# Rests of the first and the last unit multiplied as a second pair, and a new order of the last stores

## The chip, the cores and the metric

The kernel runs on one core of a Trainium2 chip. The core has five engines that run side by side, each through its own instructions in order: TensorE (PE in the profile; its weight loads are PEld), VectorE (DVE), ScalarE (ACT), GpSimd (POOL) and SyncE (SP), which here issues nearly all DMA transfers. They wait for one another by semaphores. The metric is the device time of one execution in microseconds; lower is better.

## The reference

The program is an attention block with normalized queries and keys, followed by a feed-forward layer with a squared ReLU, all in float32.

```python
batch, n_heads, seq, head_dim = (8, 12, 448, 64)
n_tokens, d_model, d_ff = (3584, 768, 2048)

def rmsnorm(x, g):
    rms = np.sqrt(np.mean(x * x, axis=-1, keepdims=True) + 1e-06)
    return x / rms * g
q_n, k_n = (rmsnorm(q, g_q), rmsnorm(k, g_k))
scores = scale * np.matmul(q_n, k_n.transpose(0, 1, 3, 2))
attn = softmax(scores)                    # written out with max, exp and sum
x = np.matmul(attn, v)                    # then (B, H, S, D) -> (B*S, H*D)
h = np.maximum(x @ w_in, 0.0)
out = h * h @ w_out
```

## The kernel before

**Units, blocks, stages.** Two batches (2 x 448 = 896 rows) make a unit; there are four, u = 0 to 3. The feed-forward layer of unit u runs while the attention of unit u+1 is computed; unit 3's runs alone at the end. The hidden width of 2048 is cut into four blocks. A block of a unit has *first products* (x @ w_in, then ReLU and square into the tiles `hid`) and *second products* (`hid` @ w_out, added into the accumulators `accs`).

**Seven products for eight.** Matrix products are done by Winograd's form of Strassen's method: four quarters are multiplied in seven products (P1 to P7, table `PRODUCTS`) of sums of quarters. In the second products of a unit, the 448 rows of one batch and the 448 of the other are the two row halves. A row tile has 128 rows, so each batch gives NT = 3 whole tiles, and the three pairs of tiles (tt = 0, 1, 2) are multiplied by `product(tt, name, ...)`: two matmuls of 128x384 (t = 0, 1) into a bank of PSUM, then one eviction (two for P7) by VectorE or ScalarE into the accumulators. The banks are three, in `roles`, turned from tile to tile. A bank is free for its next product when its eviction is done. The sums of hidden quarters (S1, S2, S4 and the changed S3) are made by POOL in `hidden_sum`, those of t = 0 during the first products, the rest after them (`make_sums`).

**Rests.** What is left of each unit is a tile of 64 + 64 rows, its *rest*. Units 1 and 2 (`KEPT`) store theirs to DRAM (`keep_rests`), and unit 3 loads both (`bring_rests`), forms their sums (`add_rests`) and multiplies them as a fourth pair, tt = NT, at the end of each block: seven products. The rests of units 0 and 3 are multiplied alone by `multiply_rest` (L1159 to L1171): eight matmuls a block. In unit 0 they come straight after the first products, under the last activations and the four POOL sums; in unit 3 they stand among the products of tile 0 (`FIRST_OF_BLOCK`).

**What sets the order.** All engines' instructions are issued in the order in which the Python code makes them. `ffn(u)` is a generator that yields a cost after each product: COST_IN = 18 for a first product of unit 0, COST_OUT = 10 for a second product. The main loop computes attention in *visits*, 24 in a unit's stage, and runs the generator between them until its summed cost reaches `place(u, x)`: in unit 0 at equal shares of COST. A visit ends in exponentials on ScalarE; the query and key transposes for the next pair (L367, on VectorE, each waiting for a transfer) are queued half a visit before.

**Weights.** In unit 0's stage the weights also have to be converted. They come as 64-bit words: `all_pieces` lists 64 pieces, per block eight `in` pieces (for the first products) and eight `out` pieces. A piece is loaded by SP into one of three buffers `words`, split by ScalarE in three steps (L1405, L1406, L1408), and joined by VectorE in two (L1419, L1438). After four pieces, sums of weight quarters are made by VectorE and POOL in turn (L1514). Each call of `convert()` joins the previous piece and splits the next; `early` and `late` list the costs at which it is called. A load is queued two steps of the generator after the conversion two pieces earlier. The derived weights for later units go to DRAM (`in_deep`, L1464, L1466, L1492) and are loaded again by `load_piece` (L892), eight or nine of these loads at the end of unit 0's last first products.

**First products of unit 0.** Seven products, twice a block, with six records each (L986). The results of P1, P5, P6 and P4 are copied by ScalarE (L995) into `part`, since the next product adds to the same bank: the copy of P1 has to be done before P6, that of P5 before P3, that of P6 before P7.

**Stores.** `store` (L1346) writes whole accumulators to `out` in the last block; in unit 3 the accumulators of tt = NT are written last, as four transfers of 64 rows.

## Time and profile before

| What | us |
|---|---|
| median of 3 runs (1391.83 to 1393.26) | 1392.92 |
| the profiled execution's own time | 1394.38 |
| its span | 1392.6 |
| stage of unit 0 (125.0 to 486.2) | 361.2 |
| stages of units 1 and 2 (486.2 to 800.0, to 1102.5) | 313.8, 302.5 |
| stage of unit 3 (to 1385.1) | 282.6 |
| from the last matmul to the end of the span | 7.5 |

A line of the profile names the source line, the engine, the operation, out<-in by the program's names, shapes and count. A timeline line begins with start and duration in us; brackets at its end hold the engine's idle time before it and what ended it. A line of waits has the waiting engine and line, what it waited for, then us in all, times and the longest. A line by stretches has start:end, its length, then busy us and instructions of PE, PEld, DVE, ACT and POOL, the granted TensorE clock, the share of time that the DMA engines were busy, and GB/s. [...] The granted clock was 1.00 in the stages of units 0, 2 and 3 and 0.99 in that of unit 1.

### The profile page before, as it was taken

How to read it: one execution, taken by the hardware profiler on the slowest of the kernel's cores; microseconds unless marked ns; L12 is line 12 of the kernel's file. 1: busy time of each engine (PE TensorE's matmuls, PEld its weight loads, DVE VectorE, ACT ScalarE, POOL GpSimd, SP SyncE). 2: the span in 40 equal slices, each digit the busy share in tenths (PEclk: the TensorE clock that was granted, in tenths of full speed). 3: DMA queues.
4: the chain of work that ended last, by engine and by line, in shares of the span. 5: the costliest groups of instructions: out<-in, count | busy, mean ns of one | idle time of the engine just before them, and what ended most of it. 6: DMA issues, size and time to landing. Idle time of an engine off the chain costs nothing.

```text
span 1392.6 us, 19474 instructions
## 1 busy us (share of the span) xinstructions
PE 1363.3 (98%) x6320; PEld 845.7 (61%) x6320; DVE 807.2 (58%) x1635; ACT 608.3 (44%) x1118; POOL 789.6 (57%) x794
## 2 busy tenths in 40 slices
PE   7999999999999999999999999999999999999997
PEld 3333444444444466676758586676768677868684
DVE  4786545867758755555556755455546642445444
ACT  6885477757666244353434244442434032202020
POOL 5668664746656868576667877566745630303030
PEclk9999999999999999999999999999999999999999
DMA  5566746968769875664739475755527442424223
GB/s 147 149 168 169 203 117 159 264 179 219 233 155 284 231 215 162 187 173 141 204 86 279 140 225 149 211 153 176 146 86 239 142 165 103 135 90 149 78 90 100
DMA packets 385588, 233.36 MB, mean 168 GB/s; under 512 B 272452, under 2 KB 354244, under 8 KB 381380
## 3 DMA queue, kind: packets, MB, share of 16 engines
q1 hardware_dynamic: 385184, 231.95, 57.7%
q8 instruction: 52, 0.85, 0.3%
q14 instruction: 60, 0.49, 0.1%
q10 hardware_dynamic: 292, 0.07, 0.0%
HBM read 174.59 MB, written 57.34 MB: 167 GB/s over the span
## 4 chain that ended last, share of the span: by engine, by line
PE 81%; POOL 4%; DVE 4%; DMA 3%; issue 3%; SPq 2%; ACT 2%; POOLq 0%; ACTq 0%; DVEq 0%
PE bank L1251 30%; PE bank L1042 20%; PE bank L986 8%; PE bank L446 5%; PE bank L536 5%; PE bank L550 4%; PE bank L435 4%; PE bank L1165 2%; POOL sum L473 2%; PE bank L585 1%; DMA qk<-in_k_dram 1%; PE bank L611 1%; SPq L326 1%; SPq L318 1%; PE bank L571 1%
## 5 line engine op out<-in xcount | busy, mean ns | idle before, releaser
L1042 PE MATMUL bank<-xT,in_sb 128*128 128x224 f32 x1344 | 289.3, 354 | 2.9 <-ACT part L1031 2.3
L1251 PE MATMUL bank<-out_sb,hid 128*128 128x384 f32 x768 | 272.5, 488 | 2.2 <-POOL out_sb L1514 1.4
L1345 DVE TENSOR_TENSOR acc<-acc,bank 128x384 f32<-128x384 f32 x312 | 166.6, 548 | 164.6 <-PE bank L1251 138.1
L1042 PEld LDWEIGHTS bank<-xT,in_sb 128*128 128x128 f32 x1344 | 252.6, 190 | 15.0 <-ACT wT L454 5.6
L454 ACT ACTIVATE wT<-bank,rr 128x448 f32<-128x448 f32 x288 | 163.5, 631 | 155.1 <-PE bank L435 92.7
L1251 PE MATMUL bank<-out_sb,sums 128*128 128x384 f32 x576 | 207.2, 490 | 1.3 <-DVE acc L1345 0.9
L1251 PEld LDWEIGHTS bank<-out_sb,hid 128*128 128x128 f32 x768 | 144.7, 190 | 104.5 <-issue 5.6
L204 POOL TENSOR_TENSOR rr<-ms,minus_half 128x8 f32<-128x8 f32 (+1 forms) x96 | 146.0, 1521 | 73.7 <-DVE ms L197 63.8
L1251 PEld LDWEIGHTS bank<-out_sb,sums 128*128 128x128 f32 x576 | 107.7, 190 | 86.3 <-issue 4.3
L1027 DVE TENSOR_TENSOR hid<-hid,bank 128x224 f32<-128x224 f32 x312 | 111.0, 383 | 83.9 <-PE bank L1042 79.1
L986 PE MATMUL bank<-xT,in_sb 128*128 128x448 f32 x336 | 131.9, 546 | 0.1
L473 POOL TENSOR_TENSOR sum<-sum,wT 128x448 f32<-128x448 f32 (+1 forms) x96 | 110.6, 1173 | 8.1 <-ACT wT L454 6.6
L986 PEld LDWEIGHTS bank<-xT,in_sb 128*128 128x128 f32 x336 | 62.1, 190 | 69.0 <-issue 60.2
L446 PE MATMUL bank<-qT,kT 64*128 64x448 f32 (+1 forms) x492 | 100.5, 571 | 1.9 <-DVE qT L409 1.1
L473 POOL TENSOR_TENSOR sum<-wT 128x448 f32<-128x448 f32 x48 | 55.8, 1183 | 69.8 <-ACT wT L454 69.8
L1099 ACT ACTIVATE hid<-hid 128x448 f32<-128x448 f32 x96 | 55.0, 573 | 66.7 <-DVE hid L1027 48.5
L435 PE MATMUL bank<-qT,kT 64*64 64x448 f32 x552 | 77.0, 547 | 1.9 <-ACT wT L454 1.9
L1042 PE MATMUL bank<-more,in_sb 128*128 128x224 f32 x288 | 76.2, 357 | 1.4 <-DVE hid L1037 1.4
L550 PE MATMUL bank<-wT,vt 64*64 64x448 f32 x576 | 74.3, 548 | 0.0
L1039 ACT COPY hid<-bank 128x448 f32<-128x448 f32 x24 | 12.8, 532 | 137.3 <-PE bank L1042 137.3
L369 ACT ACTIVATE qT<-qT,g 128x448 f32<-128x448 f32 x34 | 22.6, 665 | 113.7 <-DVE qT L367 113.7
L446 PEld LDWEIGHTS bank<-qT,kT 64*128 64x128 f32 (+1 forms) x492 | 34.9, 166 | 60.4 <-issue 36.8
(140 smaller groups left out, 2059.1 us busy)
## 6 DMA issues: line engine op xcount, KB each, us to landing
out_sb<-out_forms SPq DMA_DIRECT2D x24, 1536.0 KB, 9.9
in_sb<-in_deep SPq DMA_DIRECT2D x64, 384.0 KB, 4.2
in_sb<-in_deep SPq DMA_DIRECT2D x80, 256.0 KB, 4.1
words<-in_moe_w_in_dram SPq DMA_DIRECT2D x32, 384.0 KB, 3.8
words<-in_moe_w_out_dram SPq DMA_DIRECT2D x32, 384.0 KB, 3.6
out_forms<-out_sb SPq DMA_DIRECT2D x8, 1536.0 KB, 7.5
qk<-in_q_dram SPq DMA_DIRECT2D x96, 96.0 KB, 2.6
qk<-in_k_dram SPq DMA_DIRECT2D x96, 96.0 KB, 2.7
```

Of the source, the lines that this page charges most:

```text
L204: self.nc.gpsimd.tensor_tensor(out=self.rr[i][:, x, 0 : self.count(i)], in0=ms, in1=self.minus_half.to_broadcast(list(ms.shape)), op=ALU.pow,)
L435: nc.tensor.matmul(sc[ds(half * D, D)], lhsT=turned[i, 1][ds(e * D, D), ds(m * P + half * D, D)], rhs=turned[i, 0][ds(e * D, D), :], start ...
L446: nc.tensor.matmul(sc[some], lhsT=turned[p, 1][r, keys], rhs=turned[p, 0][r, :], start=True, stop=True,)
L454: nc.scalar.activation(new_weights((i, m), e), sc, AF.Exp, scale=rows.rr[i][:, 1, 2 * m + e : 2 * m + e + 1],)
L473: nc.gpsimd.tensor_tensor(out=sums[i, e][some], in0=left[some], in1=weights[key_of(i, m), e][some], op=ALU.add)
L536: nc.tensor.matmul(values_bank(i)[ds(e * D, D), :], lhsT=lasts[i % 2][mine, e, :] if m == NJ else values[i][:, m, e, :], rhs=weights[key_o ...
L550: nc.tensor.matmul(bank[ds(e * D, D), :], lhsT=values[i][keys, n, e, :], rhs=weights[(i, n), e][keys], start=n == 0, stop=n == NJ - 1 and ...
L986: nc.tensor.matmul(ps, lhsT=w_sb[:, IN.index(left), c, :], rhs=forms[u, c][right], start=first and c == 0, stop=c == NK - 1, skip_group_ch ...
L1027: nc.vector.tensor_tensor(out=quarter(name, n), in0=quarter(base, n), in1=ps, op=ALU.add)
L1042: nc.tensor.matmul(ps, lhsT=left, rhs=right, start=start, stop=stop, skip_group_check=True)
L1251: nc.tensor.matmul(ps, lhsT=extra[left][:, t] if tt == NT else lefts[left][:, t, ts(tt, P)], rhs=w_sb[t][:, OUT.index(right), :], start=fi ...
L1345: nc.vector.tensor_tensor(out=acc, in0=acc, in1=ps, op=ALU.add)
```

## The change

Unit 0 now keeps its rests in DRAM as units 1 and 2 do, and unit 3 has two pairs of rests, `REST_PAIRS` = ((1, 2), (0, 3)): units 1 and 2 first in each block (tt = NT), then tiles 0 and 1, then units 0 and 3 (tt = NT + 1), then tile 2. `multiply_rest` and `FIRST_OF_BLOCK` are gone. The tiles for the second pair are taken from attention's buffers wT, qT and kT; unit 3's own rest is read where it lies in `hid`. Unit 0's block cost falls from 502 to 462, and `place` divides first and second products of unit 0 into three equal parts each. The conversions of `in` pieces are spread over the second products (every 27.1 of cost), those of `out` pieces over the first 160 of 252 of the first products (every 22.5; before, all every 31.4). In the very last tile the order is P1 P2 P5 P6 P4 P7 P3 (`LAST_ORDER`): the left half of the upper rows is stored after P2, the lower rows after P7, the right half of the upper rows last.

```diff
@@ -914,8 +914,8 @@
     }
 
     FIRST_ORDER = ["P1", "P5", "P2", "P6", "P3", "P4", "P7"]
-    FIRST_OF_BLOCK = ["P1", "rest0", "P5", "P4", "P6", "P2", "rest1", "P3", "P7"]
     SECOND_ORDER = ["P1", "P2", "P5", "P6", "P4", "P3", "P7"]
+    LAST_ORDER = ["P1", "P2", "P5", "P6", "P4", "P7", "P3"]
...
     COST_IN, COST_OUT, COST_DEEP = 12 * NK // 2, 10, 3
-    COST_SECOND = (NT * 7 + 4) * COST_OUT
-    COST = NF // 2 * 7 * COST_IN + NBLK * COST_SECOND
-    COST_SHORT = NT * 7 * COST_OUT
+    COST_FIRST, COST_SHORT = 2 * 7 * COST_IN, NT * 7 * COST_OUT
+    COST = NBLK * (COST_FIRST + COST_SHORT)
     LATER = NBLK * (7 * 11 * COST_DEEP + COST_SHORT)
-    KEPT = range(1, B // 2 - 1)
-    assert len(KEPT) == 2
+    KEPT, REST_PAIRS = range(B // 2 - 1), ((1, 2), (0, 3))
+    assert B // 2 == 4
...
@@ -953,8 +952,8 @@
             ]
             second = second_products(u, blk, hid, sums_, accs)
             if u == B // 2 - 1:
-                bring_rests(blk)
-                add_rests()
+                bring_rests(blk, hid)
+                add_rests(0)
             if u:
                 yield from deep_products(u, blk, hid, sums_, second)
             else:
@@ -1150,25 +1149,8 @@
         )[n]
         nc.gpsimd.tensor_tensor(out=dst, in0=left, in1=right, op=op)
 
-    PARTS = [(0, 0), (1, 0), (0, 1), (1, 1)]
-    PARTS_BY_ROW = [(0, 0), (0, 1), (1, 0), (1, 1)]
-
     def out_of(u, blk):
         return [u * NF // 2 + 2 * blk + t for t in range(2)]
-
-    def multiply_rest(u, blk, hid, places, some, acc=None, halves=range(2)):
...
 
     def keep_rests(u, blk, hid):
 
@@ -1178,23 +1160,31 @@
                 hid[a].rearrange("p t e s -> p t (e s)")[:, :, ds(NT * P, P)],
             )
 
-    def bring_rests(blk):
+    def bring_rests(blk, hid):
 
         if not extra:
-            for name in ("11", "12", "S3", "22", "S1", "S2", "S4"):
-                some = att.tile([P, S], F32, name="wT", tag="wT", bufs=8)
-                extra[name] = some[:, 0 : 2 * P].rearrange("p (t n) -> p t n", t=2)
-            extra["accs"] = [
-                room.rearrange("p x g h d -> p (x g h d)")[:, 0:DM] for room in rows.rooms
-            ]
-        for u, names in zip(KEPT, (("11", "12"), ("S3", "22"))):
-            for a, name in enumerate(names):
-                nc.sync.dma_start(extra[name], kept[u][blk, :, a])
-
-    def add_rests():
+            tags = [["wT"] * 7, ["wT", "qT", "qT", "kT", "kT"]]
+            for n, names in enumerate((("11", "12", "S3", "22", "S1", "S2", "S4"),
+                                       ("11", "12", "S1", "S2", "S4"))):
+                some = extra[n] = {}
+                for name, tag in zip(names, tags[n]):
+                    room = att.tile([P, S], F32, name=tag, tag=tag, bufs=8 if tag == "wT" else None)
+                    some[name] = room[:, 0 : 2 * P].rearrange("p (t n) -> p t n", t=2)
+                some["accs"] = [
+                    room.rearrange("p x g h d -> p (x g h d)")[:, ts(n, DM)] for room in rows.rooms
+                ]
+        for n, us in enumerate(REST_PAIRS):
+            for u, names in zip(us, (("11", "12"), ("S3", "22"))):
+                for a, name in enumerate(names):
+                    if u in KEPT:
+                        nc.sync.dma_start(extra[n][name], kept[u][blk, :, a])
+                    else:
+                        extra[n][name] = hid[a].rearrange("p t e s -> p t (e s)")[:, :, ds(NT * P, P)]
+
+    def add_rests(n):
...
 
     def second_products(u, blk, hid, sums_, accs):
 
-        split, final = u in KEPT, u == B // 2 - 1
+        final = u == B // 2 - 1
+        split = u and not final
         if blk == 0:
-            accs.extend(new_acc() for _ in range(2 * NT if split else 2 * NT + 1))
...
@@ -1221,23 +1212,20 @@
             turn_roles(1, 2, 0)
         else:
             make_sums(0, 1, 2, 3)
-            for some in (PARTS[:3], PARTS[3:]):
-                multiply_rest(u, blk, hid, roles, some, accs[-1] if (1, 1) in some else None)
-                yield len(some) * COST_OUT
-            turn_roles(2, 1, 0)
-
-        def store_rows(tt, e):
-            if tt is None or tt == NT:
-                n = u if tt is None else KEPT[e]
+            later.append([5, lambda: keep_rests(u, blk, hid)])
+
+        def store_rows(tt, e, columns=slice(None)):
+            if tt < NT:
+                parts = [(2 * u + e, REST * e + P * tt, P)]
+            else:
+                n = REST_PAIRS[tt - NT][e]
                 parts = [(2 * n, P * NT, REST), (2 * n + 1, 0, REST)]
-            else:
-                parts = [(2 * u + e, REST * e + P * tt, P)]
-            store(accs[-1] if tt is None else accs_of(tt)[e], parts)
+            store(accs_of(tt)[e], parts, columns)
 
         def accs_of(tt):
-            return extra["accs"] if tt == NT else accs[2 * tt : 2 * tt + 2]
-
-        to_store = deque([] if split else [(None, 0)])
+            return accs[2 * tt : 2 * tt + 2] if tt < NT else extra[tt - NT]["accs"]
+
+        to_store = deque()
...
@@ -1249,7 +1237,7 @@
             role, first, left, right = PRODUCTS[name]
             for t in range(2):
                 nc.tensor.matmul(
-                    ps, lhsT=extra[left][:, t] if tt == NT else lefts[left][:, t, ts(tt, P)],
+                    ps, lhsT=lefts[left][:, t, ts(tt, P)] if tt < NT else extra[tt - NT][left][:, t],
...
@@ -1304,32 +1292,23 @@
                 if tt:
                     store_some(name)
                 yield COST_OUT
-        for tt in range(0 if split else NT + final):
-            order = SECOND_ORDER if tt or not u else FIRST_OF_BLOCK
-            for name in order:
-                if name.startswith("rest"):
-                    a = int(name[-1])
-                    multiply_rest(
-                        u, blk, hid, banks[2:0:-1], PARTS_BY_ROW[2 * a : 2 * a + 2],
-                        accs[-1] if a else None,
-                    )
-                    if a:
-                        held.discard("others")
-                    yield 2 * COST_OUT
+        for tt in () if split else (NT, 0, 1, NT + 1, 2) if final else range(NT):
+            ends = final and blk == NBLK - 1 and tt == NT - 1
+            for name in FIRST_ORDER if final and tt == NT else LAST_ORDER if ends else SECOND_ORDER:
+                product(tt, name, roles[PRODUCTS[name][0]][:, 0:HALF], nc.scalar)
+                if final and (tt, name) == (NT, "P1"):
+                    yield from sums_behind_first()
+                    add_rests(1)
                     continue
-                ps = roles[PRODUCTS[name][0]][:, 0:HALF]
-                product(tt, name, ps, nc.scalar if order is SECOND_ORDER else nc.vector)
-                if name == "P1" and order is FIRST_OF_BLOCK:
-                    yield from sums_behind_first()
-                    continue
-                if order is not FIRST_OF_BLOCK:
-                    store_some(name)
+                store_some(name)
+                if ends and name == "P2":
+                    store_rows(tt, 0, slice(0, HALF))
                 yield COST_OUT
             turn_roles(2, 0, 1)
         while to_store and blk == NBLK - 1:
             some = to_store.popleft()
             if final:
-                store_rows(*some)
+                store_rows(*some, slice(0 if some[1] else HALF, DM))
             else:
                 later.append([2, lambda some=some: store_rows(*some)])
...
-    def store(acc, parts):
+    def store(acc, parts, columns=slice(None)):
 
         at = 0
         for b, row, n in parts:
-            nc.sync.dma_start(out[ds(b * S + row, n), :], acc[at : at + n, :])
+            nc.sync.dma_start(out[ds(b * S + row, n), columns], acc[at : at + n, columns])
...
     block, tile_pieces = COST // NBLK, 4
     ahead = 4 * tile_pieces
     early = deque(2 + 2.4 * n for n in range(ahead + 1))
-    every = block / ahead
+    every = ((COST_SHORT - 2 * COST_OUT) / (ahead // 2 - 1), (COST_FIRST - 4 * COST_IN) / (ahead // 2))
     late = deque(
-        block + 2 + every * (n - 2 * tile_pieces) for n in range(len(all_pieces) - ahead)
+        n // ahead * block + (COST_FIRST, block)[m] + 2 + every[m] * (n % (ahead // 2))
+        for n in range(len(all_pieces) - ahead) for m in [n % ahead * 2 // ahead]
     )
...
     load_weights(0)
@@ -1572,13 +1552,17 @@
     def place(u, x):
 
         if u == 0:
-            return COST * x / unit
-        block = LATER // NBLK
-        second = block - COST_SHORT
-        offsets = (second * 3 // 7, second + 7 * COST_OUT, second + 18 * COST_OUT)
+            offsets = [COST_FIRST * n // 3 for n in (1, 2, 3)]
+            offsets += [COST_FIRST + COST_SHORT * n // 3 for n in (1, 2, 3)]
+            block = COST // NBLK
+        else:
+            block = LATER // NBLK
+            second = block - COST_SHORT
+            offsets = (second * 3 // 7, second + 7 * COST_OUT, second + 18 * COST_OUT)
+            x = x / VISITS
         at = [0] + [b * block + some for b in range(NBLK) for some in offsets]
-        at[-1] = LATER
-        n, more = divmod(x / VISITS, 1)
+        at[-1] = NBLK * block
+        n, more = divmod(x, 1)
         return at[int(n)] if not more else (at[int(n)] + at[int(n) + 1]) / 2
 
...
```

## The prediction

> **What bounds the kernel now.** I read the totals, then busy time by stage, then the forms of the matmuls, then the waits, and last the stretches around the edit. First the totals; columns are busy us, share of the span, instructions; the digits are tenths of forty slices.
>
> ```profile
> span 1392.6 us, 19474 instructions
> PE 1363.3 (98%) x6320; PEld 845.7 (61%) x6320; DVE 807.2 (58%) x1635; ACT 608.3 (44%) x1118; POOL 789.6 (57%) x794
> PE   7999999999999999999999999999999999999997
> PE 81%; POOL 4%; DVE 4%; DMA 3%; issue 3%; SPq 2%; ACT 2%; POOLq 0%; ACTq 0%; DVEq 0%
> ```
>
> TensorE is full in every slice but the ends, and is 81% of the chain that ended last. The stage of unit 0, that of unit 3 and the end (span, then busy us of each engine):
>
> ```profile
> 125.00:486.20 361.20, 357.85 (x1200) 164.68 (x1196) 242.29 (x434) 217.24 (x377) 225.50 (x193) 1.00 0.73 200
> 1102.50:1385.10 282.60, 282.57 (x1129) 213.05 (x1127) 129.27 (x268) 56.63 (x114) 69.93 (x72) 1.00 0.34 119
> 1385.10:1392.60 7.50, 0.00 (x0) 0.00 (x0) 1.02 (x2) 0.00 (x0) 0.00 (x0) 0.82 0.45 111
> ```
>
> A matmul record (0.49 us) is longer than the distance to the next one, so "busy" can hide lost time. The pace is read from starts:
>
> ```profile
> 177.57 5.43 PE L1165 MATMUL bank<-out_sb,hid 128*128 128x384 f32 x16
> 182.83 2.74 PE L1251 MATMUL bank<-out_sb,hid 128*128 128x384 f32 x8
> 185.41 2.74 PE L1251 MATMUL bank<-out_sb,sums 128*128 128x384 f32 x8
> ```
>
> Eight records take 185.41-182.83 = 2.58 us, 0.323 us each. One matmul of the source leaves two records: 0.645 us; a product (two matmuls) 1.29 us. The rests of one block, 16 records, take 182.83-177.57 = 5.26 us, 0.09 of it at the change of shape. Both units' stages run at this pace: unit 3 has 0.03 us without a matmul, unit 0 has 3.35 us. Three of its waits matter (us in all, times, longest):
>
> ```profile
> PE bank L1251 <- POOL out_sb L1514: 1.4, 2, 0.7
> PE bank L1251 <- DVE acc L1345: 1.0, 3, 0.5
> PE bank L446 <- ACT qT L369: 0.7, 1, 0.7
> ```
>
> [...]
>
> **The change, part by part.**
>
> *Matmuls.* Unit 0 loses 8 matmuls (16 records) per block, four blocks: 64 x 0.323 = 20.7 us out of its stage. Unit 3 loses the same 64 and gains a seven-product pair, 28 records a block: 112 x 0.323 = 36.2, net +15.5. Together 16 records: -5.2 us. Both stages are TensorE's, so all of it is on the path.
>
> *Around the pair in unit 3.* Four more evictions a block net over both units (0.55 us each on VectorE), four more POOL sums of 128x256, two more loads of 128 KB (landing in 2.1 us, the row of today's loads of rests), and two stores a block in unit 0 (2.0 us). VectorE is at 129 of 282.6 us there and POOL at 70. The first pair now heads the block: its six products after the first last 7.7 us, over the eight POOL sums (1132.7 to 1141.3 in this block) and the last activations (to 1136.8). Tile 0 needs its first sum only after P1 and P2, another 2.6 us. Cost 0; were that cover gone, about 2 us a block. In block 0 of unit 3 ScalarE, not VectorE, empties the first pair's banks: P1's copy stands behind an activation that ends at 1133.7, and P6 wants the bank at 1135.7, cost 0. SP's six loads at a block's head find the first pair's tiles free (it now heads the block, the second pair is free a tile before the end), so nothing queues behind them. The store of unit 0's rests (two issues) moves from SP's queue in block 3 to unit 3's.
>
> *Cover lost in unit 0.* The four POOL sums behind the last first-product had 5.2 us of rests over them; now tile 0 starts at once.
>
> ```profile
> 264.68 5.43 PE L1165 MATMUL bank<-out_sb,hid 128*128 128x384 f32 x16
> 265.25 1.41 POOL L1151 TENSOR_TENSOR sums<-hid 128x384 f32<-128x384 f32 x1 [4.93 <-ACT hid L1135]
> 268.79 0.99 POOL L1151 TENSOR_TENSOR hid<-hid 128x384 f32<-128x384 f32 x1
> ```
>
> This is a block with the short attention visit. From 264.7, P1 and P2 run to 267.3, after the first sum (266.7); P6 starts at 268.6, after the second (267.75); P3 at 271.2 and P7 later, after the last (269.8). Cost 0, with 0.6 us to spare; without it, up to 1 us a block.
>
> *Conversions of weights.* Eight out pieces a block used to be split at first products 1, 2, 4, 6, 8, 9, 11, 13 of 14; now at 1, 2, 3, 4, 6, 7, 8, 9. Gain: the last weight form is ready long before the second products, so the POOL wait above goes (two waits, 0.70+0.69, and the 0.16 that a record's length hides at each: 1.7). The wait of 0.7 behind L369 goes too, as no split stands before that visit, and about half of the VectorE waits (1.1 with the hidden part). Together -3.0. What is late next is the split itself. ScalarE is in order:
>
> ```profile
> 244.64 0.51 ACT L995 COPY part<-bank 128x448 f32<-128x448 f32 x1
> 245.36 0.56 ACT L1405 ACTIVATE words<-words 128x384 f32<-128x384 f32 x1 [0.21 <-DMA words<-in_moe_w_out_dram]
> 246.41 1.07 ACT L1408 ACTIVATE words<-words 128x384 f16<-128x384 f32 x1
> 247.23 0.62 ACT L995 COPY part<-bank 128x448 f32<-128x448 f32 x1
> 249.50 0.57 ACT L1405 ACTIVATE words<-words 128x384 f32<-128x384 f32 x1 [1.64 <-DMA words<-in_moe_w_out_dram]
> ```
>
> A split takes 2.1 us of a 2.26 us product (six records of 0.376), and its words land 3.6 us after an issue that waits for a buffer three pieces back. Behind a late split stand the copies of P1, P5, P6, P4, and TensorE waits for a copy two products (4.5 us) later. I laid block 1 out by hand from its start at 220.8 with these rows: the fifth load issues at about 238 (behind the five in_deep stores that now hold SP from 232 to 238) and lands at about 244, ScalarE waits 3 us for it, and the copy of the second P6 ends at 260.4 where P7 wants it at 259.8. So 0.6 us; I take 0.8 for each of three blocks, +2.4. Ends: 0 (the lag stays inside the 4.5 us) and 4 us a block (every load after the stores 2 us later, and the next two as well).
>
> *Visits and in pieces.* The visits of attention in the first products stay after products 5, 10 and 14; in the second products they move from mid-tile to the ends of tiles 0 and 1, where all banks but the last two are empty. The in pieces of the next block come every 27 cost units there instead of 31; VectorE was busy 29.5 of 36.8 us in the fullest such stretch. Taken at 0; the bound is another 1 us a block either way.
>
> *VectorE's wait for the keys in block 3.* It is in order too:
>
> ```profile
> 458.42 0.65 DVE L367 STREAM_TRANSPOSE kT<-qk 128x448 f32<-128x448 f32 x1 [4.12 <-DMA qk<-in_k_dram]
> ```
>
> The transfer stands on SP behind nine loads for unit 1 that start with the block's second products, so it lands 15 us after these start in either kernel. Before, a visit lay over the wait. After, tile 0 ends at +9.0 and the visit at +12.7; tile 1's P1 runs to +14, and its P2 wants a bank that VectorE empties at about +16. I take +2.0; ends 0 and +3.5. In the same place the DMA share rises: 11.0 MB in 42.6 us become about 11.3 in 37.4, 300 GB/s, which this trace holds for 5 us at a time (302 and 312).
>
> *The end.* SP's last issue ends at 1387.98, 2.9 us after the last matmul (1385.08); one issue there took about 1.3 instead of 0.47.
>
> ```profile
> 1384.93 3.06 SPq L1350 DMA_DIRECT2D out_dram<-qk  x3
> 1385.11 1.02 DVE L1345 TENSOR_TENSOR qk<-qk,bank 128x384 f32<-128x384 f32 x2 [0.73 <-PE bank L1251]
> ```
>
> After, P7's two evictions (1.02) lie under P3's 1.29 us, the lower rows are issued under P3, and one eviction (0.55) and one issue (0.47) follow: last issue 1.1 us after the last matmul, up to -1.8. The bytes bound it: 590 KB from +0.9 at the 188 GB/s of the last four stores (786 KB in 4.18 us) land 0.6 us before today's. I take -1.2 between 0 (the long issue and the closing waits stay) and -1.8.
>
> Sum: -5.2 -3.0 +2.4 +2.0 -1.2 = -5.0 us. The profiled execution took 1394.38 us (span 1392.6, 1.8 around it), 1.5 above the median 1392.92 of three; 1394.38-5.0 = 1389.4 for such a one, 1387.9 against the median.
>
> **Rivals.** What a measurement here can tell from no change is about 0.2%, 2.8 us.
>
> *A, slower: ScalarE's queue becomes the bound in the first products of blocks 1 to 3.* For: ScalarE is busy 21.2 of 25.0 us from 237 to 262 with splits spread out, and DMA is at 0.93 there. Against: the 4.5 us between a copy and its use. At 4 us a block it costs 12 instead of 2.4: -5.0+9.6 = +4.6, 1397.5. It decides from about 2.5 us a block (7.5 in all), where the sum is zero. The join's first step on VectorE takes 0.35 us at its shortest here and 1.17 at others. [...]
>
> *B, little left: DMA.* Block 3 at 300 GB/s delays keys, queries and forms for unit 1; keys at +3.5, the entry into unit 1 2 us later and nothing at the end: -5.2-3.0+2.4+3.5+2.0 = -0.3, 1392.6. For: 0.86 DMA share there already. Against: unit 1's first loads are issued in the same order.
>
> *C, more: the waits go and none comes.* -5.2-3.0-1.2 = -9.4, 1383.5. For: the last five first products now have no split, so the block's seam is calmer.
>
> *D: the saving isn't there.* If unit 0 were bound elsewhere, +15.5 would stand against nothing. The starts at 0.323 us exclude it but for a few per cent.
>
> **How the numbers follow.** Forecast 0.50 (1385.5 to 1390), C 0.17, B 0.18, A with D 0.15. The range takes the forecast, B's middle and C: 1383.5 to 1393.3, leaving out A and the edges. Faster by over 0.2%: the forecast and C, and a few hundredths of B, 0.70; same: the rest of B, 0.16; slower: 0.14.
>
> **What would show it.** Right: unit 0's stage shorter by 15 to 22 us, unit 3's longer by 15.5 with no waits; no wait for POOL out_sb. The fifth and sixth splits of a block preceded by waits for words of 2 to 4 us; L367 in block 3 waits for keys and TensorE for VectorE soon after, about 2 us. After the last matmul, one eviction and one issue. Wrong: waits of TensorE for "part" copies of several us in blocks 1 to 3, or a longer gap at the entry into unit 1.

## The result, and the profile after

The changed kernel takes 1396.42 us (median of 20 executions, 1393.38 to 1399.55) against 1393.6 for the kernel before on the same chips (20, 1390.45 to 1397.79): a ratio of 1.0022, 95% interval 1.0016 to 1.0028. The forecast was 1387.9 with a range up to 1393.3: the change is slower, by 0.2%, where it was called faster, and its time lies above the range. The profiled execution took 1398.04 us with a span of 1395.8, 3.2 more than the span before.

The totals of the page after: the same 98% of TensorE, 16 records fewer, and a chain that holds less of TensorE (72% of it, 81% before) and more of transfers, VectorE, POOL and ScalarE.

```profile
span 1395.8 us, 19559 instructions
PE 1362.5 (98%) x6304; PEld 843.2 (60%) x6304; DVE 815.8 (58%) x1647; ACT 607.9 (44%) x1122; POOL 802.8 (58%) x810
PE 72%; DMA 6%; issue 5%; DVE 5%; POOL 5%; ACT 4%; SPq 3%; POOLq 0%; ACTq 0%; DVEq 0%
```

By stretches: unit 0's stage, unit 3's, and the end.

```profile
125.00:474.80 349.80, 341.14 (x1136) 153.23 (x1132) 241.26 (x425) 213.95 (x375) 226.26 (x191) 1.00 0.76 208
1092.00:1390.30 298.30, 298.23 (x1177) 222.03 (x1175) 138.64 (x287) 59.31 (x120) 81.13 (x88) 1.00 0.34 118
1390.30:1395.80 5.50, 0.12 (x1) 0.00 (x0) 0.55 (x1) 0.00 (x0) 0.00 (x0) 0.95 0.33 116
```

Unit 0's stage is 349.8 us where it was 361.2. Its busy time on TensorE fell by 16.7 us, and time without any matmul rose from 3.35 to 8.66 us. Unit 3's stage has 0.07 us without a matmul: it is as full as it was.

The starts of TensorE's records mark the stages. The last column is an experiment told below (four buffers of words, the profile of its second run), put here because it shows what the same stages take when one cause is removed.

| us | before | after | after, four buffers |
|---|---|---|---|
| first products of block 0 | 48.51 | 48.47 | 48.32 |
| second products of block 0 | 43.27 | 38.11 | 38.11 |
| first, block 1 | 43.85 | 46.49 | 44.51 |
| second, block 1 | 45.87 | 41.08 | 39.84 |
| first, block 2 | 45.48 | 48.33 | 44.93 |
| second, block 2 | 43.55 | 38.42 | 38.48 |
| first, block 3 | 43.85 | 45.01 | 44.51 |
| second, block 3, to the last record's start | 42.49 | 39.52 | 38.43 |
| entry into unit 1 | 10.38 | 10.59 | 8.91 |
| units 1 and 2 | 606.25 | 606.98 | 608.57 |
| unit 3, to the last record's start | 282.05 | 297.87 | 297.87 |
| from there to the end of the span | 7.99 | 5.91 | 5.89 |
| span | 1392.58 | 1395.85 | 1388.01 |

Of what moved, unit 3 pays 15.8 us, the end gives 2.1, units 1 and 2 take 0.7, and unit 0 gives back 11.2 where its matmuls alone are worth 20.7. Of the 9.5 us that are missing, 6.7 lie in the first products of blocks 1, 2 and 3, which hold no changed matmul at all and yet take 2.6, 2.9 and 1.2 us more; 2.7 lie in the second products, most of them in block 3. Where TensorE waits (columns: us in all, times, longest; the stretch is unit 0's stage):

```profile
PE bank L602 <- ACT wT L454: 2.6, 2, 1.4
PE bank L1239 <- DVE acc L1324: 2.6, 4, 1.0
PE bank L446 <- ACT qT L369: 2.2, 4, 0.8
PE bank L985 <- ACT part L994: 1.1, 1, 1.1
```

The waits for weight forms on POOL are gone, as forecast. In their place stand waits for ScalarE, and mostly not for the copies `part`: L446 and L602 are matmuls of attention, and wait for queries (L369) and exponentials (L454) that ScalarE made late. What ScalarE itself waits for are, above all, the words of the `out` pieces; its own waits from 215 to 500 us, before:

```profile
ACT words L1405 <- DMA words<-in_moe_w_in_dram: 11.8, 6, 3.6
ACT words L1405 <- DMA words<-in_moe_w_out_dram: 7.9, 5, 4.0
```

and after:

```profile
ACT words L1384 <- DMA words<-in_moe_w_out_dram: 25.1, 7, 5.9
ACT words L1384 <- DMA words<-in_moe_w_in_dram: 11.7, 5, 3.9
```

One stretch of block 1 after the change shows the way from a load to TensorE: SyncE's queue first, then ScalarE, then TensorE, each in order of time.

```profile
227.56 0.35 SPq L1370 DMA_DIRECT2D words<-in_moe_w_out_dram  x1
228.99 3.69 SPq L1443 DMA_DIRECT2D in_deep<-in_sb  x3
232.73 2.48 SPq L1445 DMA_DIRECT2D in_deep<-in_sb  x2
235.32 1.18 SPq L1370 DMA_DIRECT2D words<-in_moe_w_out_dram  x1
...
229.69 0.56 ACT L1384 ACTIVATE words<-words 128x384 f32<-128x384 f32 x1 [2.79 <-DMA words<-in_moe_w_out_dram]
231.56 0.63 ACT L369 ACTIVATE qT<-qT,g 128x448 f32<-128x448 f32 x1
242.72 0.55 ACT L1384 ACTIVATE words<-words 128x384 f32<-128x384 f32 x1 [4.51 <-DMA words<-in_moe_w_out_dram]
251.60 2.17 ACT L454 ACTIVATE wT<-bank,rr 128x448 f32<-128x448 f32 x4
...
232.24 0.97 PE L446 MATMUL bank<-qT,kT 64*64 64x448 f32 x4 [0.44 <-ACT qT L369]
253.92 0.97 PE L602 MATMUL bank<-sum,ones 128*64 128x448 f32 x4 [1.18 <-ACT wT L454]
```

The fourth split (229.69) waits 2.79 us for its words; the queries that the visit needs stand behind it on ScalarE, and that visit of 20 records takes 4.91 us where it took 3.52 before. The load of 235.32 lands 7.4 us after its issue; the sixth split waits 4.51 us for it, ScalarE does not catch up, and the next visit's exponentials begin at 251.60 and not at 247.07, where they begin when the words are there in time. The matmul of L602 writes to a bank that held scores, and waits until the exponentials have read them, so TensorE stops at 252.7 with first products ready behind it.

### The profile page after: what moved, and what is told of

Same layout as the page of the kernel before. It is cut to its first block, busy times and chain, and to the rows that moved or that the text cites. A ratio compares the mean times of both kernels' runs of the same rounds, so it can differ in the third digit from the quotient of the medians.

```text
span 1395.8 us, 19559 instructions
## 1 busy us (share of the span) xinstructions
PE 1362.5 (98%) x6304; PEld 843.2 (60%) x6304; DVE 815.8 (58%) x1647; ACT 607.9 (44%) x1122; POOL 802.8 (58%) x810
## 4 chain that ended last, share of the span: by engine, by line
PE 72%; DMA 6%; issue 5%; DVE 5%; POOL 5%; ACT 4%; SPq 3%; POOLq 0%; ACTq 0%; DVEq 0%
PE bank L1239 32%; PE bank L1041 20%; PE bank L435 4%; PE bank L550 4%; PE bank L446 3%; DMA words<-in_moe_w_out_dram 3%; PE bank L536 3%; PE bank L985 3%; POOL sum L473 2%; DVE more L1453 1%; DMA qk<-in_k_dram 1%; PE bank L611 1%; SPq L318 1%; SPq L326 1%; DMA in_sb<-in_deep 1%
## 5 line engine op out<-in xcount | busy, mean ns | idle before, releaser
L1239 PE MATMUL bank<-out_sb,hid 128*128 128x384 f32 x800 | 285.5, 489 | 2.0 <-DVE acc L1324 2.0
L1041 PEld LDWEIGHTS bank<-xT,in_sb 128*128 128x128 f32 x1344 | 252.5, 190 | 15.7 <-ACT wT L454 5.6
L1324 DVE TENSOR_TENSOR acc<-acc,bank 128x384 f32<-128x384 f32 x300 | 159.9, 547 | 146.5 <-PE bank L1239 135.3
L454 ACT ACTIVATE wT<-bank,rr 128x448 f32<-128x448 f32 x288 | 163.8, 630 | 132.3 <-PE bank L435 92.9
L1239 PEld LDWEIGHTS bank<-out_sb,hid 128*128 128x128 f32 x800 | 149.9, 190 | 114.1 <-issue 9.0
L1094 POOL TENSOR_TENSOR hid<-hid 128x448 f32<-128x448 f32 x24 | 27.2, 1138 | 176.5 <-DVE hid L1026 172.0
L446 PE MATMUL bank<-qT,kT 64*128 64x448 f32 (+1 forms) x492 | 103.4, 571 | 3.4 <-ACT qT L369 2.2
L473 POOL TENSOR_TENSOR sum<-wT 128x448 f32<-128x448 f32 x48 | 56.1, 1187 | 68.5 <-ACT wT L454 68.5
L446 PEld LDWEIGHTS bank<-qT,kT 64*128 64x128 f32 (+1 forms) x492 | 35.1, 166 | 64.5 <-issue 36.7
```

Of the source, the lines that this page charges most:

```text
L446: nc.tensor.matmul(sc[some], lhsT=turned[p, 1][r, keys], rhs=turned[p, 0][r, :], start=True, stop=True,)
L454: nc.scalar.activation(new_weights((i, m), e), sc, AF.Exp, scale=rows.rr[i][:, 1, 2 * m + e : 2 * m + e + 1],)
L473: nc.gpsimd.tensor_tensor(out=sums[i, e][some], in0=left[some], in1=weights[key_of(i, m), e][some], op=ALU.add)
L1041: nc.tensor.matmul(ps, lhsT=left, rhs=right, start=start, stop=stop, skip_group_check=True)
L1239: nc.tensor.matmul(ps, lhsT=lefts[left][:, t, ts(tt, P)] if tt < NT else extra[tt - NT][left][:, t], rhs=w_sb[t][:, OUT.index(right), :], ...
L1324: nc.vector.tensor_tensor(out=acc, in0=acc, in1=ps, op=ALU.add)
```

## The experiments

Theory after the result: **late words**. With the out pieces every 22.5 of cost a piece is due each 3.9 us (44 us of first products for a cost of 252), the three buffers turn too slowly, and visits of attention queue behind the late splits. Rivals: the rests, while they stood ahead of tile 0, were cover for something (**lost cover**); the new places of the visits; the seventh accumulator or the order of the end.

**Out pieces at the old spacing.**

```diff
-    every = (..., (COST_FIRST - 4 * COST_IN) / (ahead // 2))
+    every = (..., COST_FIRST / (ahead // 2))
```

> The changed kernel with the out pieces converted every 31.5 of cost, as the kernel before had them, instead of every 22.5. Theory 1 (words land late for the bunched splits, ScalarE stands in order before them, and attention's exponentials and query scalings behind them make TensorE wait): the first products of blocks 1 to 3 (46.5, 48.3, 45.0 us from their first record to the first second product) go back to about 43.9, 45.5, 43.9, ScalarE's waits for words of out pieces from 25 to about 8 us; against that the last weight forms come late for tile 0, 1 to 2 us a block, so in all -2 to +1 us. Rival 2 (the rests were cover, and without them the seam and the second products stall): first products unchanged within 0.5 us a block.

It took 1404.25 us, ratio to before 1.0069 (1.0052 to 1.0086). ScalarE's waits for out words fall to 8.7 us, and the first products of blocks 1 to 3 are back at 44.19, 44.93 and 44.18 us. But the second products of blocks 1, 2 and 3 lose 6.6, 4.5 and 1.8 us against the table's column after, and not the 1 to 2 us a block that were expected. TensorE's waits in unit 0:

```profile
PE bank L1239 <- DVE out_sb L1493: 8.4, 3, 2.9
PE bank L1239 <- POOL out_sb L1493: 5.5, 2, 2.8
```

Behind two of these waits the granted clock (the number behind POOL's count) fell to a half, for 6.8 us in block 1 and 3.4 us from 361.24 in block 2:

```profile
269.08:275.91 6.83, 4.07 (x7) 2.06 (x7) 2.23 (x4) 2.92 (x4) 6.38 (x6) 0.50 0.91 245
```

TensorE was busy for 4.1 and 3.4 us of these stretches, and half of that, an estimated 2.0 and 1.7 us of the 6.6 and 4.5, is the clock and not the wait itself (the last section has more of this). The mean granted clock of all four executions is 0.994 to 0.995, and 0.998 to 1.0 for the changed kernel.

The two lines of waits are for sums of weight quarters that tile 0 needs. Before, they were as late as here (POOL's last one ends 56.4 us after block 1's first record, here 56.1), but 16 records of rests (5.2 us) stood between the last first product and tile 0. So both theories hold a part: the rests were cover for the weight forms, and without them the out pieces must be early; early pieces need their words early.

**The kernel before, rests kept, with the new spacing alone.**

The list `late` takes the changed kernel's formula for it.

```diff
-    every = block / ahead
+    first_of = 2 * 7 * COST_IN
+    every = ((COST_SECOND - 2 * COST_OUT) / (ahead // 2 - 1), (first_of - 4 * COST_IN) / (ahead // 2))
```

> The kernel before, its rests kept in the first unit, with one thing of the change: the out pieces of the weights' conversion every 22.5 steps of cost and not every 31.4. If the spacing alone makes the words late, ScalarE waits for them as long as after the change (some 37 us in place of 20) and TensorE loses 4 to 8 us behind it: 1398 to 1402 us. If the spacing only hurts together with the shorter blocks, the waits stay near 20 us and the time near 1393.9 us, and can even fall by up to 1.4 us, as the weight forms that tile 0 waited for are ready earlier.

It took 1395.36 us, 1.0012 (1.0003 to 1.0021). ScalarE's waits (215 to 500 us) double, as after the change:

```profile
ACT words L1405 <- DMA words<-in_moe_w_out_dram: 27.5, 8, 4.9
ACT words L1405 <- DMA words<-in_moe_w_in_dram: 12.0, 4, 5.1
```

The first products of blocks 1 to 3 take 1.5, 2.1 and 1.3 us more than before, with no rests moved and attention's visits placed by the old formula; the second products give 1.5 back in sum, 1.7 of it in block 1, where tile 0 no longer waits for weight forms. The late words are therefore made by the spacing alone; the price in the time was smaller than the 4 to 8 us expected, since 4.9 us of loss stand against this gain. The four kernels side by side:

| median us (ratio to before) | out pieces every 31.4 or 31.5 | every 22.5 |
|---|---|---|
| rests in unit 0 | 1393.6 | 1395.36 (1.0012) |
| rests in unit 3 | 1404.25 (1.0069) | 1396.42 (1.0022) |

By the ratios, moving the rests (with the rest of the change) at the old spacing costs 9.6 us; the new spacing takes back 6.5 of them there, and costs 1.7 where the rests stay.

**A spacing between.** `COST_FIRST - 2 * COST_IN` in place of `- 4 * COST_IN`: every 27.

> The kernel after the change with its out pieces every 27 steps of cost, between its own 22.5 and the 31.5 that took 1404.3 us. Words would be less late (waits of 10 to 15 us for out pieces, not 25), the weight forms for tile 0 later by 5 us. If the two costs trade evenly: 1396 to 1399 us; if the late forms start only beyond this spacing, the words' gain shows: 1392 to 1394 us; if forms are late at once: 1400 us and more.

1398.21 us, 1.0031 (1.0019 to 1.0043): the even trade. The waits for out words are 20.2 us in place of 25.1, and a wait of 1.9 us for POOL's weight forms is back. With three buffers no spacing tried escapes.

**Four buffers of words.** The fourth takes the room of the seventh accumulator, which was left over once the rests had gone from unit 0; loads are asked for three pieces ahead.

```diff
-        return ffn_p.tile([P, HALF, 2], U32, name="words", tag="words", bufs=3)
+        return ffn_p.tile([P, HALF, 2], U32, name="words", tag="words", bufs=4)
...
-        to_load.append([2, n + 2])
+        to_load.append([2, n + 3])
...
     load_weights(1)
+    load_weights(2)
...
-        return ffn_p.tile([P, DM], F32, name="acc", tag="acc", bufs=2 * NT + 1)
+        return ffn_p.tile([P, DM], F32, name="acc", tag="acc", bufs=2 * NT)
```

> The changed kernel with four buffers for words instead of three (one accumulator buffer fewer, which unit 0 no longer needs) and each load queued one piece further ahead. It takes away the late landing and leaves the cadence of the splits. Theory 1: ScalarE's waits for out words fall from 25 us to under 8, first products of blocks 1 to 3 lose 4 to 6 us in all, time about 1391 to 1393 where the changed kernel has 1396.5. If instead ScalarE's own load (2.1 us of split per 2.26 us product) is the cause, the waits for words go but the first products stay within 1.5 us of what they are. Rival 2: no change of time.

1390.88 us, 0.9973 (0.9962 to 0.9984). It was run again beside other kernels:

> The kernel with four buffers of words and loads three pieces ahead once more, to be compared on one chip with the three others: 1390.9 +- 0.8 us, 0.9973 of the time before.

1389.52 us, 0.9966 (0.9953 to 0.9979). It beats both kernels: by the medians 5.5 to 6.9 us under the changed one, and 3 to 5 under the one before on the same chip. ScalarE's waits for words (215 to 500 us) in the second run:

```profile
ACT words L1384 <- DMA words<-in_moe_w_in_dram: 3.3, 3, 1.3
ACT words L1384 <- DMA words<-in_moe_w_out_dram: 0.5, 1, 0.5
```

and the same place in block 1, exponentials and the matmul behind them:

```profile
247.07 2.21 ACT L454 ACTIVATE wT<-bank,rr 128x448 f32<-128x448 f32 x4 [0.41 <-PE bank L446]
...
252.37 0.97 PE L602 MATMUL bank<-sum,ones 128*64 128x448 f32 x4
```

TensorE no longer waits at L602. The table's last column shows where the time came back: 2.0, 3.4 and 0.5 us in the first products of blocks 1 to 3, 2.3 in the second products. Whether a fourth buffer would help the kernel before was not tried: the room that it takes here is that kernel's seventh accumulator. TensorE had 3.35 us without a matmul in that kernel's unit 0, so there was little for it to take away.

**The control: six accumulators, three buffers.** Only the last line of the diff above.

> The kernel after the change with six accumulators in place of seven, and nothing else: the other half of what was edited for the four buffers of words (1390.88 us). Theory of the late words: the seventh accumulator is not what held the kernel up, so 1396.4 +- 1.0 us, and ScalarE still waits some 25 us for the words of the out pieces and 12 for those of the in pieces in the first unit. Rival, the ring of accumulators did it (other addresses, stores that wait otherwise): 1391 to 1393 us.

1397.76 us, 1.0024 (1.0014 to 1.0035): a third of a microsecond over the expected band, the changed kernel's ratio (1.0022) within its interval, and far from 1391; waits for words 23.8 and 17.4 us. The accumulator had no part in it.

**Four buffers, loads two pieces ahead as in the changed kernel.**

> Six accumulators and four buffers of words, but each load asked for as late as in the kernel after the change, two pieces ahead and not three. Theory A, the loads stood in SyncE's queue for a buffer that was still being read: with a fourth buffer they go at once, ScalarE's waits for words fall from 37 us to under 12, and the time is 1391 to 1393 us. Theory B, the loads were asked for too late whatever the buffers, or stood behind other DMA issues: the waits stay above 25 us and the time within 1 us of 1396.4.

1392.99 us, 0.9988 (0.9979 to 0.9996), with 15.7 and 10.5 us of waits for words. Against the control, the fourth buffer alone takes 15 of 41 us of waits and 0.36% of the time (5 us): loads had stood in SyncE's queue for a buffer still in use. Asking one piece sooner, in the two runs above, takes another 22 us of waits and 0.15 to 0.22% (2 to 3 us). Neither theory has it alone.

**Stores of raw forms spread.** Behind the five `in_deep` stores (6.2 us of issue above) stood the load of 235.32.

```diff
-        return [raw] + [lambda make=make: both(make) for make in steps + [None, None]]
+        return [lambda make=make: both(make) for make in steps + [None, None]]
...
         def both(make):
+            if raw:
+                n, some = raw.popleft()
+                nc.sync.dma_start(keep[:, :, PLACES[n]], some)
```

> The kernel after the change, three buffers of words, with the five stores of raw first-layer forms that each of blocks 1 to 3 issues in one step at its beginning (6.2 us on SyncE's queue, 228.99 to 235.21, and a load of words right behind them) handed out one per step, and the derived forms' stores one step sooner. Theory, these stores are what the load two pieces ahead stands behind: ScalarE's waits for words of out pieces fall from 25 us to 15 or less, and the time by 2 to 4 us, to 1392.5 to 1394.5. Rival, the load waits for a free buffer, or lands late whoever is ahead of it (7.4 us to landing): the waits stay above 20 us and the time within 1 us of 1396.4.

1396.2 us, 1.0015 (1.0006 to 1.0024): no different from the changed kernel. The waits for out words are 20.8 us and those for in words rose to 18.1. The load is issued at 231.63 there, but the next one still at 241.91: SyncE's queue stands still for 3.8 us until VectorE's join (L1417) has read the buffer. SyncE's wait from 236 to 243 us:

```profile
SPq L1370 <- DVE out_sb L1417: 3.8, 1, 3.8
```

The stores in front of the load were seen in the trace, but moving them away brings no time.

**Visits spread evenly**, as the formula before the change has it, first on the changed kernel and then on the one with four buffers.

```diff
         if u == 0:
-            offsets = [COST_FIRST * n // 3 for n in (1, 2, 3)]
-            offsets += [COST_FIRST + COST_SHORT * n // 3 for n in (1, 2, 3)]
-            block = COST // NBLK
+            return COST * x / unit
```

> The changed kernel with attention's visits at equal shares of unit 0's cost, as before, instead of at the ends of tiles. Theory 1: the first products keep their loss (visits there are after nearly the same products), time within 1.5 us of the changed kernel. Rival 3 (visits at tile ends put the stalls where they hurt): unit 0's stage 3 us shorter or more.

1408.83 us, 1.0104 (1.0085 to 1.0124): 12.4 us over the changed kernel, and not within 1.5 as expected. In its trace the third visit of a block, which before lay by chance of the costs (251 of 252) behind the last first product, lies ahead of that product's records; then the second products follow at once on the products whose hidden sums they need. TensorE, then POOL, in block 1:

```profile
261.29 2.52 PE L985 MATMUL bank<-xT,in_sb 128*128 128x448 f32 x6
263.64 3.08 PE L1239 MATMUL bank<-out_sb,hid 128*128 128x384 f32 x8
267.97 0.91 PE L1239 MATMUL bank<-out_sb,sums 128*128 128x384 f32 x2 [0.60 <-POOL sums L1150]
...
266.91 1.00 POOL L1150 TENSOR_TENSOR sums<-hid 128x384 f32<-128x384 f32 x1 [4.96 <-ACT hid L1134]
```

The first 24 records of second products take 1.3 us too long in block 0 and 2.8 in each of blocks 1 to 3. The kernel with four buffers tells what the same spread costs when the words are in time:

> The kernel with four buffers of words (1389.5 to 1390.9 us) with attention's visits spread evenly over the first unit's blocks, as before the change. With three buffers that spread cost 12.4 us. In its trace the third visit of a block stands ahead of the last 6 matmuls of the first products and no longer behind them, and each block's second products begin 2.6 us late, waiting for POOL's sums. If this lost cover is the larger part: 8 to 11 us more than with four buffers, 1398 to 1401 us. Rival, the spread hurts by the late words behind it: within 3 us, 1390 to 1393 us.

1398.25 us, 1.0031 (1.002 to 1.0042): 7.4 to 8.7 us over four buffers alone. So more than half of the price is there without late words. Not all of it is the seam. In this profile, against four buffers alone, the second products of the four blocks take 8.8 us more, block 0's first products 1.2 less, and the entry into unit 1 takes 4.0 more (there TensorE waits 3.79 us for exponentials in place of 2.12). The granted clock fell to a half behind a wait in block 2, for 3.4 us, and during the one at the entry, for 6.8; with TensorE busy for 3.4 and 4.8 us of it, half of that is an estimated 4 us. The seam begins the loss; how the rest divides between late words, visits and clock was not separated.

**The old end.** The last tile in the old order, whole rows stored.

```diff
-            for name in FIRST_ORDER if final and tt == NT else LAST_ORDER if ends else SECOND_ORDER:
+            for name in FIRST_ORDER if final and tt == NT else SECOND_ORDER:
...
-                store_rows(*some, slice(0 if some[1] else HALF, DM))
+                store_rows(*some)
```

> The changed kernel with the old end: products of the last tile in the usual order, P7 last, whole rows stored after it. The traces put the end at 8.0 us from the last product's last record before and 5.9 after. If the new order and the halves make that difference, this is 1.5 to 2.1 us slower than the changed kernel; if the last tile being a whole tile (two stores of 128 rows instead of four of 64) makes it, 0 to 0.5 us slower.

1397.22 us, 1.0022 (1.0012 to 1.0031). The ratio is the changed kernel's, so the executions show no gain from the new order. In the profile the old end takes 6.62 us from the last record's start, between 7.99 before and 5.91 after. By these single profiles the new order and the halves make 0.7 of the 2.1 us, and the last tile being a whole one (two stores of 128 rows in place of four of 64) the other 1.4; but the same new end takes 5.89 to 6.37 us in the other kernels, so the 0.7 is hardly clear of their spread.

**Forms of the second layer loaded later.** With four buffers, unit 1 waits for a first-layer form that lands 13.4 us after its issue, beside two loads of 1536 KB (the first run's profile). Besides the line below, the list `later` is gone through so that an entry that is due no longer stands behind one that is not.

```diff
-        later.append([4, lambda: [load_out(n + 2) for n in ns]])
+        later.append([16 if blk == NBLK - 1 else 4, lambda: [load_out(n + 2) for n in ns]])
```

> The kernel with four buffers of words and three pieces ahead (1390.88 us) in which the two loads of second-layer forms that are issued at the end of a unit (1536 KB each) go 16 steps after it and not 4. In that kernel unit 1 began 18.5 us earlier than before the change, but took 312.0 us where it took 309.6: TensorE waited 2.7 us for a first-layer form whose load landed 13 us after its issue, beside those two loads. Theory, the loads of 3 MB take the DMA engines from the form that is needed first: the wait goes, unit 1 takes 309.5, and the time is 1388 to 1389 us, under the kernel with four buffers by 2 to 3 us. Rival, SyncE's short attention loads of the first unit hold the queue and not the bytes: no change from 1390.9 us, the wait stays above 2 us.

1390.67 us, 0.9978 (0.9968 to 0.9987). The wait does go, as the theory has it, and unit 1 takes 310.4 us, 1.1 less; but the time stays within the two runs of the kernel without the edit (1390.88 and 1389.52). Entry and unit 1 together take 321.15 us in this profile and 320.45 without the edit. The last section shows what stood in the way in this profile.

## Why the prediction was wrong

It failed at one step, "*Conversions of weights*", twice over: the split's lag was put at 2.4 us and measured 6.7, and the waits that were to give 3.0 us made room for others (the three lines of the prediction add up to 3.1 us before, and to 4.8 after). Each of the other steps came out within about 1 us.

- **Matmuls, -5.2.** Right. Unit 3 pays 15.8 for 15.5. Unit 0's second products fall by 18.0 us after the change and by 20.3 with four buffers, for 20.7. Rival D is out.
- **Around the pair in unit 3, 0.** Right: 0.07 us without a matmul in the stage, and 297.86 to 297.89 us in every kernel with the pair.
- **Cover lost in unit 0, 0 for POOL's sums.** Right for the kernel as changed: TensorE waits nowhere for `sums`. The 0.6 us to spare came from the visit at the seam. Without that visit the first 24 records lose 1.3 us in block 0 and 2.8 in the others, part of it in waits for VectorE, where I gave "up to 1 us".
- **The cover that I did not name.** I let the weight forms' wait go because the pieces move forward, and did not say that the rests were cover for them. The out pieces at the old spacing show it: 8.4 and 5.5 us of waits.
- **Waits that go, -3.0.** POOL's waits for forms went (1.4 to 0), but those for VectorE rose from 1.0 to 2.6 and those behind L369 from 0.7 to 2.2. The wait of 0.7 was at the end of block 2's first products, and I argued that without a split before that visit it goes. The last split there now ends 11 us ahead of the queries, and the wait is still 0.69 (350.65): the queries stand on ScalarE behind the last activations of `hid`, for which ScalarE waits 2.84 us on VectorE, until 347.78. So the split had not been its cause. The other three are new; the first is at the fourth split of block 1, late by 2.79 us. With four buffers what is left of the three lines is 1.5 us.
- **The split's lag, +2.4 (ends 0 and 4 a block).** This is the mis-sized term. The first products of blocks 1 to 3 lost 2.64, 2.85 and 1.17 = 6.7 us, inside the ends, nearly three times what I took; against the kernel with four buffers 2.0, 3.4 and 0.5 = 5.9. The mechanism was rival A's. Two blocks passed A's point of decision, 2.5 us; in sum it stayed under A's 7.5, and the waits that did not go made up the rest. That A's time of 1397.5 lies near the measured one is partly luck: A had the lag at 12 us and the waits gone. I followed the lag to the wrong place: to the copies `part` and their 4.5 us of slack, where TensorE waited 1.1 us in all. What stands behind a late split on ScalarE is also attention's scaling and exponentials, and the visits had no such slack here. The waits that I forecast for the fifth and sixth splits (2 to 4 us) were there in block 1, 2.79 and 4.51, but at the fourth and the sixth. The joins did not get dearer when bunched: their first step took 0.52 us on average for out pieces between 215 and 480 us (L1398), and 0.69 before (L1419).
- **VectorE's keys in block 3, +2.0.** Right in place, and in the sum of the block: its second products fall by 2.97 us where the matmuls alone are worth 5.17 (16 x 0.323). But only about half is the keys. VectorE's wait, then two of TensorE:

```profile
450.04 0.65 DVE L367 STREAM_TRANSPOSE kT<-qk 128x448 f32<-128x448 f32 x1 [5.11 <-DMA qk<-in_k_dram]
...
443.96 1.56 PE L1239 MATMUL bank<-out_sb,hid 128*128 128x384 f32 x4 [0.98 <-DVE acc L1324]
451.18 1.56 PE L1239 MATMUL bank<-out_sb,hid 128*128 128x384 f32 x4 [0.81 <-DVE acc L1324]
```

The record of 451.18 is the wait foretold, and starts 1.1 us late; the one of 443.96 lies ahead of the keys, 1.1 us late too, behind VectorE's other work. With four buffers the keys come as late (VectorE waits 4.57 us) and TensorE waits 0.7 us in all: rival B's mechanism is there, and small.

- **The end, -1.2 (0 to -1.8).** -2.1, a little beyond the end of the range: one issue and one eviction follow the last product, as told, and the two last issues take 1.16 us together. I had not counted that the last tile became a whole one, which by the profiles is the larger part; the executions with the old end are no slower, so the -1.2 for the new order is not shown.

```profile
1388.97 1.45 PE L1239 MATMUL bank<-out_sb,sums 128*128 128x384 f32 x4
1390.21 1.16 SPq L1329 DMA_DIRECT2D out_dram<-acc  x2
1390.46 0.55 DVE L1324 TENSOR_TENSOR acc<-acc,bank 128x384 f32<-128x384 f32 x1 [0.27 <-PE bank L1239]
```

- **The sum.** Unit 0 was to give 20.7 + 3.0 - 2.4 - 2.0 = 19.3 us and gave 11.2: of the difference of 8.1, 3.0 is in the second products (-18.0 where -20.7 - 2.3 + 2.0 = -21.0 was meant), 4.9 in the first (+6.6 where 2.4 of lag less the 0.7 behind L369 was meant), 0.2 in the entry. With the words in time unit 0 gives 20.6 in the second run's profile, 1.5 of it at the entry (the last section has why), and the kernel takes 1389.5 to 1390.9. The weighing of rivals was wrong with it: A with D got a part of 0.15, and what spoke for A, the load that waits "for a buffer three pieces back", stood in my own step.

With four buffers the second products of unit 0 take 20.3 us less, for 20.7 of matmuls taken out, so unit 0 is TensorE's, and the starts at 0.323 us told it rightly.

## What to carry to other kernels

When work that "only" fills time is moved away, ask what it covered: here 5.2 us of rests a block hid late weight forms, and the remedy for that brought the next lateness. When steps of an in-order engine are drawn together, compare their new period (3.9 us) with how fast their buffers come round, and follow the lag to everything queued behind, other streams first: here TensorE waited 1.1 us in all for the copies `part`, and 2.6 and 2.2 us for attention's exponentials and queries. A buffer freed by the same change may be worth more than the change. And a wait on TensorE can cost more than its length, by the clock that follows it: behind one of 2.1 us, 28 records took 4.85 us in place of 3.15.

## What the runs showed of the hardware that was not expected

Behind a short gap TensorE lost an estimated 1.7 us more, at half its clock. At the entry into unit 1 TensorE waits 1.9 to 2.3 us for exponentials in most of these kernels. In the kernel after, the granted clock (the number behind POOL's count) was still whole for 0.3 us behind this gap, then a half for 3.4 us, then whole again:

```profile
478.10:480.20 2.10, 0.04 (x2) 0.00 (x0) 0.86 (x2) 1.20 (x3) 2.09 (x2) 1.00 0.63 143
480.20:480.52 0.32, 0.28 (x4) 0.21 (x8) 0.00 (x0) 0.32 (x1) 0.25 (x1) 1.00 0.02 3
480.53:483.93 3.40, 3.40 (x24) 1.21 (x18) 0.00 (x0) 1.85 (x4) 3.40 (x4) 0.50 0.19 58
483.95:485.10 1.15, 1.15 (x13) 0.21 (x5) 0.00 (x0) 0.69 (x2) 1.07 (x2) 1.00 0.56 91
```

The kernel before has the same from 492.18 us, 0.8 us behind its gap and for 3.4 us, and so has the one with the forms loaded later:

```profile
473.10:476.40 3.30, 3.30 (x19) 1.02 (x12) 0.00 (x0) 1.61 (x4) 3.22 (x4) 0.50 0.41 106
```

With four buffers, second run, the clock stayed whole behind the same gap of 2.1 us:

```profile
472.50:475.70 3.20, 3.16 (x29) 1.18 (x29) 0.00 (x0) 2.89 (x5) 3.14 (x3) 1.00 0.30 83
```

The 28 records of attention behind the gap take 4.85 us with the fall and 3.15 without. That is the 1.7 us by which the entry differs in the table, half of 3.4, and why loading the forms later gained nothing in its profile: the wait of 2.1 us for the form in unit 1 went, but at the entry the clock fell. Gaps of 2.1 us with and without the fall stand side by side; a gap of 1.89 us, before, was followed by one, and a gap of 2.69 us in the first run with four buffers (to 515.9) was not. So the length of the gap alone does not decide it here. Each of these falls lasted 3.4 us or twice that. What decides it in these kernels was not tried.

So of the 7.8 us between the spans after and with four buffers, an estimated 1.7 are this clock and no merit of the words. The gain in the medians does not show as a gain in clock: the mean granted clock is on record for every execution to three digits, and a fall of 3.4 us to a half lowers it by an estimated 0.001 (1.7 in some 1390). It is 0.998 or 0.999 in the five executions of the second run, whose times do not part by it (1389.13 and 1390.13 us at 0.998, 1389.15 to 1389.91 at 0.999), and 0.997 to 0.999 in those of the kernel before on the same chip.
